# A hand-written plan of 1,494 steps is put into a new order on every engine

## The chip, the core and the metric

The kernel runs on one core of a Trainium2 chip. A core has five engines with a queue each: TensorE (PE, with its weight loads shown apart as PEld), VectorE (DVE), ScalarE (ACT), GpSimd (POOL) and SyncE (SP, which issues DMAs). Each takes its instructions in the order in which the program gives them, and waits on semaphores for the other engines. The metric is the device time of one execution in microseconds, and less is better.

## The reference

Inputs are `q`, `k`, `v` of shape (8 batches, 8 heads, 576 positions, 64), float32. First a linear attention with a "hedgehog" feature map, then a gate with a long convolution over the positions:

```
phi(x):  p = x @ w_phi (64 -> 128);  p -= max|p| per row;  [exp(p), exp(-p)]
kv = phi(k)^T v ; z = sum phi(k) ; attn = (phi(q) kv) / (phi(q) z)
x  = attn, heads side by side              # (8, 576, 512)
x1, x2, x3 = split(x @ w_proj)             # 512 -> 3 x 512
conv = irfft(rfft(x2) * rfft(filter_fft))  # along the 576 positions
out  = (x1 * conv * x3) @ w_out
```

## The kernel before

The kernel handles the eight batches one after another in a software pipeline: while the convolution of batch b runs, the attention of batches b+1 and b+2 is on its way. Everything is bfloat16 with float32 accumulation in PSUM, which has eight banks; most steps use a pair of them.

A batch goes through these steps (b is the batch, v or m one of four tiles of 128):

- `load` brings `q`, `k`, `v` in over POOL's DMA queue; `trh` transposes q and k by DMA on SP. For batch 0 `pt` (PE) and `pte` transpose instead, and `loadh` loads halves.
- `Qn`, `Pk` (PE) project q and k; `maxq`, `maxk` (DVE, line 710) reduce the absolute maximum; `ex` (ACT, line 696) takes the exponentials straight from PSUM. `Pq` projects q a second time, transposed, with the maximum (`mhi`, `mlo`, `trm`, `trme`) subtracted.
- `em` (ACT) and `vs` (POOL, line 752, `vp` and `vm`) scale v; `KV` (PE) sums k-features times v; `NE` (PE, line 781) applies it to q; `rc`, `xn` (DVE) divide. A small remainder of the positions goes the same way under names with a t (`Pkt`, `NEt`, `rct`, `xnt`).
- `trx`, `trxt` (SP) transpose the result by DMA to `xT`; `X1`, `X3` (PE, line 922) multiply with two thirds of `w_proj`.
- `f1` (line 849, `SD<-xn`) and `f2` (line 855, `xf<-SD`) are the butterfly sums ahead of the Fourier transform; each is on POOL or DVE. `F` (PE, lines 861 and 865) is the transform, `Fe` copies it out, `Xl` gathers a rest, `X2` (PE, line 900) multiplies with the last third of `w_proj`, `Y1` (DVE, lines 905, 910) multiplies with the filter's spectrum, and `m3` (line 914, `T<-T,T`) adds two products.
- `I` (PE, line 975) goes back to positions; `Ie` (ACT), `Ip` and `Im` (DVE, line 996) form sums and differences `cv`; `tm` (DVE) multiplies x1 and x3; `ym` (line 1041, `yT<-cv,x1s`) is the gate, on POOL or DVE; `J` and `yj` (line 1035) do the same for one tile with another transform. `yt` copies the rest.
- `O` (PE, line 1052) multiplies with `w_out`, `Oe` copies to one of four buffers `o0` to `o3`, `st` stores half a buffer from SP or, for the last batch, also from ACT.

Ahead of this the kernel makes the Fourier matrices from counters (`ang`, `frac`, `sin`), the filter's spectrum (`fl_load`, `fa`, `rev`, `fb`, `Ff`, `H`, `He`), and a few small constants (`one`, lines 354 and 355). `wz` steps (line 317) are matmuls on zeros whose result nobody reads.

Nothing is scheduled by the compiler: the text `PLAN` lists the steps, `name,arguments@bank`, and `run` calls them in this order, so the plan is the order of every queue and the choice of bank, and for many steps the first argument is the engine. Semaphores come from the data that the steps touch, so another order does the same work and waits in other places.

Of the kernel before, what the change touches and what calls it, by code (L numbers as in the profile page):

```python
# [37 lines left out]
wz,2@2 maxq,0,0@4 pt,q,0,1,0@0 sin,2 Pk,0,0@1 pte,ACT,q,0,1,1@3 fa,POOL,1 pt,k,0,1,0@6 maxk,0,0@1
pte,ACT,q,0,1,0@0 Qn,0,2@4 pt,k,0,1,1@0 maxq,0,2@4 pt,k,0,0,1@3 ex,k,p,0,0@1 load,k,1
pte,DVE,k,0,1,1@0 Qn,0,3@4 pte,DVE,k,0,1,0@6 ex,k,m,0,0@1 fa,POOL,0 wz,9@0 one Pk,0,3@6 maxq,0,3@4  # L40
pte,ACT,k,0,0,1@3 Pk,0,2@0 ex,k,m,0,3@6 Qnt,0@2 Pk,0,1@4 maxqt,0@2 ex,k,p,0,3@6 maxk,0,1@4 rev@2
ex,k,p,0,2@0 maxk,0,3@6 ex,k,p,0,1@4 maxk,0,2@0 Pkt,0@6 mhi,0 ex,k,m,0,1@4 trh,q,1,0 mlo,DVE,0
maxkt,0@6 ex,k,m,0,2@0 trm,0@4 wz,24@5 trme,DVE,0@4 fb,0@2 fl_loadt Pq,0,1@4 exkt,p,0@6 trh,q,1,1
exkt,m,0@6 wz,28@0 em,m,0,0 em,p,0,0 em,p,0,1 ex,q,m,0,1@4 vs,DVE,m,0,0 vs,POOL,p,0,0 Pq,0,2@6
ex,q,p,0,1@4 trh,k,1,0 fb,1@2 Pq,0,3@0 ex,q,m,0,2@6 Qn,1,0@4 wz,5@2 maxq,1,0@4 ex,q,m,0,3@0
trh,k,1,1 ft,POOL KV,0,0@2 ex,q,p,0,2@6 load,q,2 vs,DVE,p,0,1 em,m,0,1 ex,q,p,0,3@0 Qn,1,3@4
vs,POOL,m,0,1 maxq,1,3@4 Pk,1,1@6 KVe,ACT,0,0@2 Ff,0@0 ex,k,p,1,1@6 NE,0,1@2 Pq,0,0@4 Ffe,ACT,0@0
rc,0,1@2 gen_ends,POOL xn,0,1@2 ex,q,m,0,0@4 Pk,1,0@0 maxk,1,1@6 KV,0,1@2 trx,0,1 ex,q,p,0,0@4
load,v,1 maxk,1,0@0 ex,k,m,1,1@6 w_load,proj,2 NE,0,0@4 KVe,DVE,0,1@2 ex,k,m,1,0@0 load,k,2
rc,0,0@4 NE,0,2@2 xn,0,0@4 ex,k,p,1,0@0 Ff,1@6 rc,0,2@2 f1,POOL,0,0,1 xn,0,2@2 Qn,1,2@4 Ffe,ACT,1@6  # L50
ptx,0,0@0 maxq,1,2@4 Pqt,0@2 ptxe,ACT,0,0@0 f1,POOL,0,0,0 NE,0,3@6 exqt,p,0@2 Ff,3@0 rc,0,3@6
exqt,m,0@2 Ff,2@4 xn,0,3@6 Ffe,ACT,3@0 Pkt,1@2 f2,DVE,0,0,0 f1,POOL,0,1,1 Ffe,ACT,2@4 ptx,0,3@6
maxkt,1@2 Qn,1,1@0 ptxe,ACT,0,3@6 NEt,0@4 maxq,1,1@0 exkt,m,1@2 ptx,0,2@7 w_load,proj,1 exkt,p,1@2
ptxe,DVE,0,2@7 Hl,ACT f2,POOL,0,0,1 Qnt,1@0 Pk,1,2@2 maxqt,1@0 X1,0,2@7 ex,k,m,1,2@2 rct,0@4
f1,POOL,0,1,0 xnt,0,0@4 Pk,1,3@0 xnt,0,1@4 em,m,1,0 X1,0,3@6 ex,k,m,1,3@0 maxk,1,2@2 f2,POOL,0,1,0
# [6 lines left out]
vs,POOL,m,1,1 ex,k,m,2,1@0 late Y1,0,2@5 X2,0,3@6 ex,k,m,2,0@2 X1,0,1@0 mlo,DVE,1 load,k,3
ex,k,p,2,0@2 Y1,0,3@6 X2,0,1@5 load,q,3 Xl,ACT,0 trm,1@1 X3,0,1@2 Y1,0,0@4 trme,ACT,1@1 m3,POOL,0,1
X1e,ACT,0,1@0 Pq,1,1@6 Y1,0,1@5 Pkt,2@0 X2,0,4@4 ex,q,m,1,1@6 maxkt,2@0 m3,POOL,0,0 X3,0,0@5
ex,q,p,1,1@6 Y1,0,4@4 X1t,0@3 tm,0,1@2 exkt,m,2@0 X3t,0@4 exkt,p,2@0 tm,0,0@5 Pq,1,0@6 em,p,2,0
w_load,out X1te,ACT,0@3 Qn,2,3@0 tmt,0@4 KV,1,1@2 ex,q,p,1,0@6 vs,POOL,p,2,0 maxq,2,3@0
ex,q,m,1,0@6 Pq,1,2@4 KVe,DVE,1,1@2 Qn,2,1@0 ex,q,m,1,2@4 NE,1,0@6 maxq,2,1@0 load,k,4 X3,0,2@2
# [6 lines left out]
f1,POOL,1,1,1 NEt,1@4 trx,1,3 Oe,ACT,0,0@1 f1,DVE,1,1,0 O,0,3@0 ex,k,p,2,3@2 maxqt,2@6
f2,POOL,1,1,0 O,0,2@1 rct,1@4 xnt,1,0@4 ex,k,m,2,3@2 xnt,1,1@4 f2,DVE,1,1,1 Ft,1,1,6@4 trxt,1
em,m,2,1 Oe,DVE,0,2@1 em,p,2,1 Qn,3,2@2 Fs,1,3@6 maxq,3,2@2 Fs,1,2@4 X1,1,3@1 Fe,ACT,1,3@6
st,SP,0,1,0 Fe,ACT,1,2@4 trh,k,3,1 F,1,0@6 X1e,ACT,1,3@1 F,1,1@4 Oe,ACT,0,3@0 Qn,2,2@1 Fe,ACT,1,0@6
Fe,DVE,1,1@4 st,SP,0,3,1 X1,1,2@0 maxq,2,2@1 trh,k,3,0 X2,1,0@4 X2,1,2@5 mhi,2 X1e,ACT,1,2@0
st,SP,0,0,1 mlo,POOL,2 vs,POOL,m,2,1 st,SP,0,2,0 trm,2@0 X3,1,0@1 Y1,1,2@5 trme,ACT,2@0 trh,q,3,0
# [1038 lines left out]
```

## Time and profile before

| what | value |
|---|---|
| time, median of the runs | 311.26 us |
| lowest of the runs | 310.44 us |
| span of the profiled execution, first to last instruction | 309.5 us |
| median less span (what lies around the span) | 1.8 us |
| PE busy | 281.9 us, 91% |
| DVE busy | 270.8 us, 88% |
| ACT busy | 219.7 us, 71% |
| POOL busy | 201.8 us, 65% |

The profile is of one execution. The page gives busy time by engine; the groups give the mean duration of each kind of instruction; the windows give busy time in a stretch; the timeline shows the rows one after another, where rows of a kind that follow each other are merged ("x3"). An idle time in square brackets stands with what ended it.

### The profile page before, as it was taken

The page shows a single profiled execution, that of the slowest core. Times are in us where ns is not written, and L with a number is a line of the kernel's source. Part 1 is how long each engine was busy: PE and PEld are TensorE (multiplying, and loading weights), DVE is VectorE, ACT ScalarE, POOL GpSimd, SP SyncE. Part 2 cuts the span into 40 slices and gives each one's busy share as a digit, 9 for nine tenths or more (in the row PEclk, how much of TensorE's full clock was granted, in tenths as well). Part 3 has the DMA queues.
Part 4 walks back from the last instruction along what each step waited for, and adds up shares of the span by engine and source line. Part 5 has one row for each costly group of instructions (what it writes and reads, how often), then busy time and mean ns, then how long its engine had stood idle before and what let it go on. Part 6 is the DMA issues. An engine that isn't in the chain of part 4 may idle for free.

```text
span 309.5 us, 10297 instructions
## 1 busy us (share of the span) xinstructions
PE 281.9 (91%) x4337; PEld 203.6 (66%) x4364; DVE 270.8 (88%) x451; ACT 219.7 (71%) x354; POOL 201.8 (65%) x160
## 2 busy tenths in 40 slices
PE   8558888999999999999599899899999999999993
PEld 3333657688568777676358767577487766886661
DVE  6999999999979896999899897878999888797963
ACT  1988999896749895899338768977657898924120
POOL 8253879998558748949445369957699619773040
PEclk9977999999999999999799999999999999999998
DMA  7999799999599994999929976962756142041236
GB/s 147 229 208 180 97 173 162 147 210 178 89 181 200 132 182 108 135 142 159 179 27 216 131 105 135 160 113 59 114 130 118 32 103 54 2 69 32 65 78 196
DMA packets 72191, 40.07 MB, mean 129 GB/s; under 512 B 52496, under 2 KB 66960, under 8 KB 72144
## 3 DMA queue, kind: packets, MB, share of 16 engines
q1 hardware_dynamic: 56928, 22.49, 40.2%
q0 software_dynamic: 14816, 16.25, 33.4%
q8 instruction: 34, 0.56, 0.8%
q10 hardware_dynamic: 400, 0.66, 0.7%
q14 instruction: 13, 0.11, 0.1%
HBM read 33.75 MB, written 9.44 MB: 140 GB/s over the span
## 4 chain that ended last, share of the span: by engine, by line
PE 72%; DVE 12%; issue 5%; ACT 5%; DMA 4%; POOL 0%; SPq 0%; DVEq 0%; POOLq 0%; ACTq 0%
PE ps L922 16%; PE ps L900 10%; PE ps L1052 8%; PE ps L767 6%; PE ps L781 5%; PE ps L975 5%; DMA xT<-xn 3%; PE ps L931 3%; PE ps L1031 3%; PE ps L861 2%; PE ps L641 2%; PE ps L668 2%; PE ps L865 2%; PE ps L634 2%; PE ps L674 2%
## 5 line engine op out<-in xcount | busy, mean ns | idle before, releaser
L922 PE MATMUL ps<-xT,wproj 128*128 128x256 bf16 x512 | 64.9, 273 | 0.8 <-DMA xT<-xn 0.8
L922 PEld LDWEIGHTS <-wproj 128*128 128x128 bf16 x512 | 48.5, 98 | 11.4 <-issue 1.8
L752 POOL TENSOR_TENSOR vp<-vn,vp 128x1152 bf16<-128x1152 bf16 x15 | 33.3, 2228 | 23.6 <-ACT vp L746 23.4
L710 DVE TENSOR_REDUCE mq<-ps 128x8 f32<-128x1024 f32 (+1 forms) x40 | 43.9, 1112 | 5.0 <-PE ps L649 2.6
L710 DVE TENSOR_REDUCE mk<-ps 128x8 f32<-128x1024 f32 (+1 forms) x40 | 44.0, 1111 | 2.7 <-PE ps L649 1.8
L1041 POOL TENSOR_TENSOR yT<-cv,x1s 128x576 bf16<-128x576 f32 x23 | 29.1, 1280 | 21.8 <-DVE cv L996 19.9
L849 POOL TENSOR_TENSOR SD<-xn 128x512 bf16<-128x512 bf16 x23 | 26.6, 1167 | 23.0 <-DVE xn L800 22.1
L752 POOL TENSOR_TENSOR vm<-vn,vm 128x1152 bf16<-128x1152 bf16 x15 | 32.9, 2191 | 8.4 <-ACT vm L746 8.4
L696 ACT ACTIVATE Eqm<-ps 128x1024 bf16<-128x1024 f32 x32 | 32.4, 1027 | 6.7 <-PE ps L674 6.6
L696 ACT ACTIVATE Ekp<-ps 128x1024 bf16<-128x1024 f32 x32 | 32.8, 1038 | 4.5 <-DVE mk L710 3.0
L1052 PE MATMUL ps<-wout,yT 128*128 128x512 bf16 x131 | 34.9, 387 | 1.2 <-issue 0.4
L696 ACT ACTIVATE Eqp<-ps 128x1024 bf16<-128x1024 f32 x32 | 32.6, 1029 | 3.8 <-PE ps L674 3.6
L696 ACT ACTIVATE Ekm<-ps 128x1024 bf16<-128x1024 f32 x32 | 32.9, 1035 | 1.8 <-PE ps L634 1.5
L900 PE MATMUL ps<-wproj,XF 128*128 128x512 bf16 x121 | 30.0, 379 | 0.6 <-issue 0.3
L914 POOL TENSOR_TENSOR T<-T,T 128x1024 bf16<-128x1024 bf16 x13 | 27.6, 2131 | 4.1 <-DVE T L910 4.1
L298 ACT CAST x1s<-ps 128x512 bf16<-128x512 f32 (+1 forms) x31 | 16.3, 536 | 17.5 <-PE ps L931 9.7
L910 DVE TENSOR_TENSOR T<-ps,HTo 128x1024 bf16<-128x1024 f32 x16 | 19.5, 1219 | 5.0 <-PE ps L900 5.0
L855 POOL TENSOR_TENSOR xf<-SD 128x512 bf16<-128x512 bf16 x19 | 21.9, 1167 | 2.8 <-DVE SD L849 2.4
L800 DVE TENSOR_TENSOR xn<-ps,r 128x512 bf16<-128x512 f32 x32 | 22.0, 690 | 1.1
L963 DVE TENSOR_TENSOR x1s<-ps,x1s 128x512 bf16<-128x512 f32 x32 | 21.4, 682 | 0.9 <-ACT XF L298 0.5
L1052 PEld LDWEIGHTS <-yT 128*128 128x128 bf16 x144 | 13.3, 99 | 13.4 <-issue 1.4
L298 ACT COPY o<-ps 128x512 f32<-128x512 f32 x24 | 14.4, 601 | 9.4 <-PE ps L1052 9.4
(179 smaller groups left out, 689.7 us busy)
## 6 DMA issues: line engine op xcount, KB each, us to landing
out_dram<-o SPq DMA_DIRECT2D x67, 128.0 KB, 2.5
vn<-in_v_dram POOLq DMA_DIRECT2D x8, 576.0 KB, 8.1
qn<-in_q_dram POOLq DMA_DIRECT2D x7, 576.0 KB, 8.1
kn<-in_k_dram POOLq DMA_DIRECT2D x7, 576.0 KB, 8.5
wproj<-in_moe_w_proj_dram POOLq DMA_DIRECT2D x3, 512.0 KB, 10.1
fl<-in_moe_filter_fft_dram SPq DMA_DIRECT2D x8, 128.0 KB, 6.4
out_dram<-o ACTq DMA_DIRECT2D x5, 128.0 KB, 2.9
qn<-in_q_dram POOLq DMA_DIRECT2D x2, 288.0 KB, 7.1
```

The source lines that it names most:

```text
L298: self.nc.scalar.copy(dst, src)
L696: self.nc.scalar.activation(e, p, AF.Exp, bias=0.0, scale=1.0 if g == "p" else -1.0)
L710: self.nc.vector.tensor_reduce(out=out, in_=src, axis=AX.X, op=ALU.max, apply_absolute_value=True)
L752: self.eng(eng).tensor_tensor(out=t[:, :, :, 0:64], in0=self.at("vn", b)[:, 2 * X:2 * X + 2], in1=t[:, :, :, 64:65].to_broadcast([128, 2, ...
L800: self.nc.vector.tensor_tensor(out=o, in0=n[:, :, :, 0:64], in1=self.at("r", 4 * b + v).to_broadcast([128, 2, 4, 64]), op=ALU.mult)
L849: self.eng(eng).tensor_tensor(out=o[:, :, 2 * i:2 * i + 2, :], in0=x[:, :, 0:2, :], in1=x[:, :, 2:4, :], op=ALU.subtract if i else ALU.add)
L855: self.eng(eng).tensor_tensor(out=o[:, :, 2 * i:2 * i + 2, :], in0=x[:, :, 0:4:2, :], in1=x[:, :, 1:4:2, :], op=ALU.subtract if i else ALU ...
L900: self.mm(self.pb(0), l, w[:, kt, 512:1024], start=(kt == 0), stop=(kt == 3))
L914: self.eng(eng).tensor_tensor(out=Y, in0=Y, in1=self.at(f"T{2 * e + 1}", b), op=ALU.add)
L922: self.mm(o[:, d], w[:, kt, f0 + 128 * m:f0 + 128 * m + 128], y[:, 1, ::-1, ::-1] if d else y[:, 0], start=(kt == 0), stop=(kt == 3))
L1041: self.eng(eng).tensor_tensor(out=self.at("yT", b)[:, m, 0:SEQ], in0=self.turn_of("cv", (b, m)).rearrange("p x h t -> p (x h t)"), in1=sel ...
L1052: self.mm(self.pb(0), y[:, kt, 128 * c:128 * c + 128], w[:, kt, :], start=(kt == 0), stop=(kt == 3))
```

## The change

Only the table `PLAN` changes. It holds as many steps as before, 1,494, and the same work: the same 16 `wz` steps and the same loads and stores. What differs is the order, on all five queues; the PSUM banks that many steps use; and the engine of 78 steps that copy, add or multiply (`Fe`, `Oe`, `X1e`, `KVe`, `Xl`, `f1`, `f2`, `m3`, `ym`, `mlo`, `trme`, `vs`, `yt`). On DVE the net is: `ym` 1 to 4 steps, `m3` 3 to 5, `f1` 9 to 10, `f2` 13 to 11, `trme` 3 to 6, `Oe` 12 to 13, `Xl` 3 to 4, and one less of `X1e`, `KVe` and `yt`. Of the loads of the filter (`fl_load`) most stand in the text behind the first loads of q and k.

```diff
-fl_load,0,1 gz,DVE loadh,q,0,0 zeros wz,14@0 w_load,phi gi_part loadh,k,0,0 wz,17@1 ident cols_m
...
+fl_loadt fl_load,0,0 w_load,phi gi_part gz,DVE wz,5@0 wz,27@1 cols_m zeros cols_i fl_load,3,0
+loadh,q,0,0 ident pt,q,0,0,0@1 loadh,k,0,0 fl_load,1,0 gi_nr ang,3 pt,q,0,0,1@0 fl_load,3,1 cols_f
...
```

Three places show what moves. Row numbers of the source are three lower in the changed kernel, since its table is three lines shorter (L855 before is L852 after). The first place is DVE in the convolution of batch 3: `SD` is written by `f1`, `xf` by `f2`, `cv` by `Ip` and `Im`, `mk` by `maxk`, `rt` and `xnt` by `rct` and `xnt`. Before:

```order
L710 TENSOR_REDUCE mk_85<-ps 128x2x4
L996 TENSOR_TENSOR cv_1121<-es_1119,ps 128x9x32 x2
L1035 TENSOR_TENSOR yT_1122<-ps,x1s_140 128x2x9x32
L300 CAST x1s_140<-ps 128x2x8x32
L849 TENSOR_TENSOR SD_136<-xn_129 128x2x256
L855 TENSOR_TENSOR xf_137<-SD_136 128x2x256 x3
L806 RECIPROCAL rt_128<-ps 128x8
L812 TENSOR_TENSOR xnt_131<-ps,rt_128 64x256 x2
```

And in the changed kernel, for the same batch:

```order
L993 TENSOR_TENSOR cv_1134<-es_1132,ps 128x9x32
L993 TENSOR_TENSOR cv_1133<-es_1131,ps 128x9x32
L846 TENSOR_TENSOR SD_136<-xn_129 128x2x256
L993 TENSOR_TENSOR cv_1133<-es_1131,ps 128x9x32
L707 TENSOR_REDUCE mk_85<-ps 128x2x4
L993 TENSOR_TENSOR cv_1134<-es_1132,ps 128x9x32
L852 TENSOR_TENSOR xf_137<-SD_136 128x2x256
L993 TENSOR_TENSOR cv_1134<-es_1132,ps 128x9x32
L1032 TENSOR_TENSOR yT_1135<-ps,x1s_140 128x2x9x32
L803 RECIPROCAL rt_128<-ps 128x8
```

One `f2` of batch 3 is left on DVE instead of three, and it and the one `f1` now stand among the half sums of batch 2. The second place is POOL beside it, with its DMA issues. Before:

```order
L1041 TENSOR_TENSOR yT_1122<-cv_1120,x1s_140 128x576
L1041 TENSOR_TENSOR yT_1122<-cv_1121,x1s_140 128x576
L593 DMA qn_75<-in_q_dram 128x4x576
L593 DMA vn_80<-in_v_dram 128x4x576
L752 TENSOR_TENSOR vp_106<-vn_79,vp_106 128x18x64
L855 TENSOR_TENSOR xf_137<-SD_136 128x2x256
```

In the changed kernel:

```order
L911 TENSOR_TENSOR T_1126<-T_1126,T_1127 128x1024
L590 DMA vn_79<-in_v_dram 128x4x576
L846 TENSOR_TENSOR SD_136<-xn_129 128x2x256 x3
L852 TENSOR_TENSOR xf_137<-SD_136 128x2x256
L1038 TENSOR_TENSOR yT_1135<-cv_1134,x1s_140 128x576
L1038 TENSOR_TENSOR yT_1135<-cv_1133,x1s_140 128x576
L590 DMA qn_75<-in_q_dram 128x4x576
L852 TENSOR_TENSOR xf_137<-SD_136 128x2x256
```

The butterflies of batch 3 have gone from DVE to POOL, and the load of v and an `m3` stand ahead of them there. The third place is the end of ACT's queue, where `o0` to `o3` are the output buffers and each DMA stores half of one. Before:

```order
L298 COPY o2_1126<-ps_61 128x512
L298 COPY o3_1127<-ps_61 128x512
L1061 DMA out_0_dram<-o3_1127 64x512
L1061 DMA out_0_dram<-o0_1124 64x512
L1061 DMA out_0_dram<-o1_1125 64x512
L1061 DMA out_0_dram<-o2_1126 64x512
L1061 DMA out_0_dram<-o3_1127 64x512
```

In the changed kernel, where DVE fills `o3`, `o0` and `o2` ahead of the last copy:

```order
L295 COPY yT0_1135<-yT1_1136 128x4x64
L1058 DMA out_0_dram<-o0_1137 64x512
L295 COPY o1_1138<-ps_61 128x512
L1058 DMA out_0_dram<-o3_1140 64x512
L1058 DMA out_0_dram<-o1_1138 64x512
L295 COPY o3_1140<-ps_61 128x512
L1058 DMA out_0_dram<-o2_1139 64x512
L1058 DMA out_0_dram<-o3_1140 64x512
```

In both the last copy (into `o3`) reuses the buffer of the first output tile of batch 7. Before, half of that tile was ACT's first store; now the store stands behind another store and behind a copy that waits for PE.

More of the change, by code (lines that the diff above doesn't have):

```diff
@@ L38 @@
[L38 to L43, printed above, removed]
@@ L62 @@
[L62 to L67, printed above, removed]
@@ L74 @@
[L74 to L79, printed above, removed]
@@ new lines @@
+Fe,ACT,0,3@4 mlo,DVE,1 w_load,out vs,POOL,m,1,1 He,ACT,1,1@2 He,DVE,4,0@1 X1,0,2@0 X1e,ACT,0,2@0
+Pk,2,1@4 KV,1,0@6 load,v,2 Pk,2,0@0 He,ACT,1,0@2 maxk,2,1@4 em,p,1,1 X3,0,0@3 trm,1@2 Xl,DVE,0
+maxk,2,0@0 trxt,0 KVe,ACT,1,0@6 ex,k,p,2,1@4 X2,0,2@6 late trme,DVE,1@2 X2,0,1@2 ex,k,m,2,1@4
+X3,0,1@7 X2,0,3@4 load,k,3 ex,k,m,2,0@0 ex,k,p,2,0@0 Y1,0,2@6 tm,0,0@3 Pq,1,1@5 Y1,0,1@2
+ex,q,p,1,1@5 tm,0,1@7 ex,q,m,1,1@5 Pkt,2@0 trh,q,2,0 trh,q,2,1 load,q,3 maxkt,2@0 X1t,0@2 X2,0,0@3
+Y1,0,3@4 exkt,m,2@0 X1te,ACT,0@2 X2,0,4@7 exkt,p,2@0 vs,POOL,p,1,1 Y1,0,0@3 KV,1,1@4 m3,POOL,0,1
```

298 lines of the change are left out of this document (153 added, 145 removed).

## Prediction

> **What bounds the kernel now.** I read the busy times first, then stretches of time, then who waited for whom, and last the rows around the worst wait.
>
> ```profile
> span 309.5 us, 10297 instructions
> PE 281.9 (91%) x4337; PEld 203.6 (66%) x4364; DVE 270.8 (88%) x451; ACT 219.7 (71%) x354; POOL 201.8 (65%) x160
> ```
>
> PE and DVE are both nearly full. The work is the same in the changed kernel, so the time can only change where PE stands idle or runs at a lower clock, which is at most 309.5 - 281.9 = 27.6 us. The windows (PE, PEld, DVE, ACT, POOL busy, then granted clock and DMA share) say where that is:
>
> ```profile
> 0.00:50.00 50.00, 38.31 (x552) 23.36 (x556) 45.08 (x103) 40.99 (x63) 31.78 (x39) 0.93 1.03 175
> 50.00:140.00 90.00, 88.20 (x1502) 66.31 (x1509) 81.67 (x125) 71.49 (x117) 68.65 (x51) 1.00 0.95 153
> 140.00:150.00 10.00, 6.28 (x66) 4.72 (x64) 9.92 (x13) 6.86 (x11) 8.39 (x7) 0.98 0.99 163
> 150.00:160.00 10.00, 9.80 (x70) 5.89 (x72) 8.83 (x12) 4.41 (x9) 4.86 (x3) 0.85 0.44 88
> 160.00:300.00 140.00, 134.97 (x2135) 101.56 (x2146) 122.40 (x198) 95.02 (x155) 88.08 (x63) 1.00 0.55 96
> ```
>
> Start-up (first 50 us) leaves PE idle 11.7 us, and part of its 38.31 us are the zero matmuls. The steady part, 230 us, leaves only 1.8 + 5.0 = 6.8 us. One window of 10 us loses 3.7 us by itself, with DVE full, and the clock falls behind it. PE's longest wait and the rows of DVE, POOL and PE there:
>
> ```profile
> PE ps L861 <- DVE xnt L812: 3.8, 1, 3.8
> 143.35 0.43 DVE L849 TENSOR_TENSOR SD<-xn 128x512 bf16<-128x512 bf16 x1
> 143.81 5.27 DVE L855 TENSOR_TENSOR xf<-SD 128x512 bf16<-128x512 bf16 x3
> 149.23 0.43 DVE L812 TENSOR_TENSOR xnt<-ps,rt 64x256 bf16<-64x256 f32 x1
> 143.44 0.81 POOL L593 DMA_DIRECT2D qn<-in_q_dram  x1
> 144.24 0.75 POOL L593 DMA_DIRECT2D vn<-in_v_dram  x1
> 145.00 2.17 POOL L752 TENSOR_TENSOR vp<-vn,vp 128x1152 bf16<-128x1152 bf16 x1
> 147.10 1.35 POOL L855 TENSOR_TENSOR xf<-SD 128x512 bf16<-128x512 bf16 x1
> 150.15 0.66 PE L861 MATMUL ps<-Dt,xnt 128*128 128x288 bf16 x2 [3.82 <-DVE xnt L812]
> L855 DVE TENSOR_TENSOR xf<-SD x13: 371/416/3649, 43.3 to 254.1; 128x512 bf16<-128x512 bf16 x13
> ```
>
> Three `f2` of batch 3 took 5.27 us on DVE, though one has a median of 0.416 us (the last row: minimum, median, maximum in ns): the first sat for 3.649 us while POOL went through two load issues and a `vs`. DVE was held, `rct` and `xnt` stood behind it, and `F` on PE waited 3.82 us. I call this a hold.
>
> **The hold goes: -5.3 us.** In the changed plan two of the three `f2` are POOL's, and those ahead of `xnt` now stand among half sums. Without the hold, three `f2` (1.25 us), `rct` and two `xnt` (1.1 us) from 143.8 end at 146.1, about when PE ran out of work (150.15 - 3.82 = 146.33), so the whole 3.82 us goes. The clock of 0.85 in the next 10 us cost 0.15 x 10 = 1.5 us more. Bounds: -3.8 (the clock falls for another reason) to -5.3; I take -5.3.
>
> The Trainium skill, page TensorE: Matmul & The Clock Gate, section Part 1: The HAM clock gate (the "warmup" mystery), says that PE drops to half clock after an idle window of about 3.4 us. The trace agrees: a wait of 3.82 us is followed by the window at 0.85. By that rule shorter waits lose only themselves.
>
> **Holds come back elsewhere: +2.5 us.** What was held was an addition on DVE with both inputs in SBUF, against POOL. Counted in the change, such steps (`f1`, `f2`, `m3`, `ym`) go from 26 to 30 on DVE. At batch 3 POOL's queue now has, in a row, `m3`, a load, three `f1`, an `f2` and a `ym`: by the rows below 2.13 + 0.8 + 3 x 1.17 + 1.17 + 1.28 = 8.9 us without a break, and DVE's `f1` and `f2` of batch 3 arrive in it. Each waits at most for the operation under way, about 1.2 us, so 2 x 1.2 = 2.4 us. From below 0 (POOL has run ahead and is free); from above a repeat of the hold, 5.3. I take 2.5, nearer to the rows of the train itself.
>
> ```profile
> L914 POOL TENSOR_TENSOR T<-T,T 128x1024 bf16<-128x1024 bf16 x13 | 27.6, 2131 | 4.1 <-DVE T L910 4.1
> L849 POOL TENSOR_TENSOR SD<-xn 128x512 bf16<-128x512 bf16 x23 | 26.6, 1167 | 23.0 <-DVE xn L800 22.1 <-DVE yT L300 0.9
> L1041 POOL TENSOR_TENSOR yT<-cv,x1s 128x576 bf16<-128x576 f32 x23 | 29.1, 1280 | 21.8 <-DVE cv L996 19.9 <-DVE x1s L967 1.6
> L914 DVE TENSOR_TENSOR T<-T,T 128x1024 bf16<-128x1024 bf16 x3 | 2.0, 680 | 0.0
> L1041 DVE TENSOR_TENSOR yT<-cv,x1s 128x576 bf16<-128x576 f32 x1 | 0.8, 759 | 0.0
> L300 DVE COPY o<-ps 128x512 f32<-128x512 f32 x12 | 8.2, 686 | 2.4 <-PE ps L1052 2.0 <-DMA out_dram<-o 0.3
> L849 DVE TENSOR_TENSOR SD<-xn 128x512 bf16<-128x512 bf16 x9 | 3.7, 424 | 0.1
> ```
>
> The Trainium skill, page SBUF — State Buffer, section Who interferes with whom, says that a VectorE instruction with two SBUF inputs contends with a GpSimd instruction that reads SBUF, and infers that generating DMA descriptors does not hold such a one. The rows agree on the first and speak against the second: the `f2` issued at 143.81 was still held from 143.81 to 145.00, when POOL did nothing but issue loads. By the page's inference loads ahead of a DVE step cost nothing, and the train above would be 0.8 us shorter.
>
> **DVE gets more work: +3.0 us.** Net of the 78 steps, DVE gains two `m3` (2 x 0.68 = 1.36) and three `ym` (3 x 0.76 = 2.28), and one `f1` more against two `f2` less is -0.42. The copies cancel at about 0.69 each, and three small `trme` less a `KVe` end near nothing. Sum +3.2 us. POOL's relief hides: no PE wait on POOL is over 0.3 us. DVE's 3.2 us could hide in its 38.7 us of idle time, hence bounds 0 to 3.2. I take 3.0, since from 50 to 140 us DVE is busy 81.67 of 90 us while PE has only 1.8 us idle, so little is hidden.
>
> **The end: +1.8 us.** The rows there (the copies to `o`, a store from ACT, and what a store takes):
>
> ```profile
> 299.07 0.76 DVE L1035 TENSOR_TENSOR yT<-ps,x1s 128x576 bf16<-128x576 f32 x1
> 299.88 4.48 PE L1052 MATMUL ps<-wout,yT 128*128 128x512 bf16 x20 [0.15 <-DVE yT L1035]
> 300.94 0.59 ACT L298 COPY o<-ps 128x512 f32<-128x512 f32 x1 [0.59 <-PE ps L1052]
> 301.56 4.21 ACTq L1061 DMA_DIRECT2D out_dram<-o  x5
> 304.55 0.69 DVE L300 COPY o<-ps 128x512 f32<-128x512 f32 x1 [0.27 <-DMA out_dram<-o]
> DMA to landing us min/median/max: 2.2/2.7/3.1
> ```
>
> Before, PE waited 0.15 us for the last `yj` and began the five `O` of batch 7 at 299.88; the buffer of the first was stored from ACT at 301.56, 1.7 us on, and the last copy began at 304.55, 4.67 us on, 0.27 us late. In the changed plan a `ym` on DVE (0.76) stands ahead of the last `yj`, after the last `I`, which delays that `O` by about 0.9 us. And the first buffer's second half is stored by ACT only behind another store, which waits for the second copy: 1.06 + 2 x 0.86 + 0.69 less the overlap puts that first store at 2.6, so the one for `o3` at 3.2, landing 2.7 later at 5.9 instead of 4.67, less 0.3 at the faster landings: +0.9. Together 1.8; bounds 0.5 (only the `ym`, half hidden) to 2.8 (a landing of 3.1 and both copies late).
>
> **The start: -0.5 us.** Before, the constant `one` was held on DVE, too, by POOL's `fa`, and PE waited behind it:
>
> ```profile
> 18.00 2.15 DVE L354 TENSOR_TENSOR onex<-ident 128x36 bf16<-128x36 bf16 x1
> 17.75 2.36 POOL L491 TENSOR_TENSOR turn<-fl 128x1024 f32<-128x1024 f32 x1
> 16.94 1.02 ACT L696 ACTIVATE Ekp<-ps 128x1024 bf16<-128x1024 f32 x1
> 2.43 4.13 SPq L479 DMA_DIRECT2D fl<-in_moe_filter_fft_dram  x7
> PE ps L634 <- DVE mq L710: 1.9, 1, 1.9
> ```
>
> Now `one` comes early, when POOL computes nothing: -1.9. Against that, two counters stand ahead of POOL's first load, and ACT has one more copy ahead of the first exponential (16.94 before), some +1.4. Whether the loads of the filter stand before or behind in the text is of little account: SP issued all of them by 6.56 us without waiting for POOL, and SP's order has them first in both. Their price I bound from the first 50 us: -3 to +2.
>
> **All other places: 0.** The steady part's 6.8 us of idle time could vanish or double: -6.8 to +6.8. No row says which, so I take nothing.
>
> Sum: -5.3 + 2.5 + 3.0 + 1.8 - 0.5 = +1.5 us on the profiled 309.5, so a span of 311.0. The median of the runs is 1.8 us above the span; carried over, 312.8 us.
>
> **Rivals.**
>
> *No new hold, and a shorter start.* -5.3 from the old hold, +0.5 at the end, -3 at the start and DVE's work hidden: 311.3 - 7.8 = 303.5 us. For it: 28 of the 31 additions and SBUF copies on DVE found POOL idle or won, so the order before mostly kept them apart. Against: four more of them, with POOL trains as long.
>
> *A hold that halves the clock.* The slower case: a DVE addition comes upon the POOL train of batch 3, or the similar one of batch 5 (`m3`, three `f1`, two `f2`), and `Ip`, `Im` and `xnt` stand behind it. It decides once PE idles over about 3.8 us, as at 146: each such place costs 5.3. With two of them, 311.3 - 5.3 + 10.6 + 3.0 + 1.8 = 321.4 us. For it: DVE is 91% busy and cannot catch up. Against: arrivals are spread, and two holds of 1.2 us stay below that point.
>
> *The filter loads do nothing.* If "behind the first inputs" were real, the inputs would land sooner; by SP's rows it is not. The time is the forecast's, 312.8; I give it 0.8 and it does not change the sum.
>
> **Chances.** The forecast and what lies within 2% of 311.3 (305.0 to 317.5) has 0.50, the first rival 0.15, the second 0.35. Two per cent, 6.2 us, is about what a measurement of this kernel can tell from no change. The range takes in both rivals and the bounds of the steady part as far as they are likely: 304 to 323.
>
> **What would show it.** Right: no PE wait near 3.8 us; DVE rows L846, L852, L1038 or L911 longer than twice their median beside POOL rows; DVE busy near 274 us; the last copy waiting for a DMA over 0.5 us; `one` under 0.5 us. Wrong: PE idle in 50 to 300 us clearly under 5 or over 15 us, or a start that is more than 3 us off.

## The result: 9% slower, and DVE's SBUF steps now meet POOL's

The changed kernel took 341.6 us (median of four runs, 338.6 to 347.5), the kernel before beside it 313.5 us (310.4, 311.3, 315.6 and one run of 462.2): a ratio of 1.094, with a 95% interval of 1.087 to 1.101. Forecast was 312.8 us with a range of 304 to 323. The profiled execution is the longest of the four (345.7 us; the others span 336.8 to 340.6), so the sums made on it are about 6 us too large for the median.

The page after, and the windows that were shown of before (PE, PEld, DVE, ACT, POOL busy, then granted clock and DMA):

```profile
span 345.7 us, 10288 instructions
PE 293.5 (85%) x4332; PEld 209.6 (61%) x4364; DVE 296.5 (86%) x457; ACT 220.3 (64%) x353; POOL 195.9 (57%) x156
```

```profile
0.00:50.00 50.00, 33.86 (x479) 21.68 (x483) 40.72 (x93) 35.78 (x51) 25.43 (x35) 0.90 1.13 172
50.00:140.00 90.00, 78.30 (x1163) 57.40 (x1171) 81.81 (x110) 62.51 (x105) 57.88 (x43) 0.94 0.76 122
140.00:150.00 10.00, 8.31 (x69) 4.35 (x68) 10.00 (x11) 4.55 (x7) 5.43 (x3) 1.00 1.22 188
150.00:160.00 10.00, 9.27 (x288) 7.96 (x287) 8.61 (x15) 6.23 (x8) 2.87 (x2) 1.00 0.50 75
160.00:300.00 140.00, 126.03 (x1888) 91.17 (x1903) 121.60 (x176) 98.13 (x161) 89.70 (x65) 0.98 0.61 101
```

Of the 36.2 us between the two profiles, 24.6 us are more idle time of PE (52.2 against 27.6) and 11.6 us are longer busy time of PE for the same matmuls, most of it at a lower clock. In a profile of the same order with one store moved (337.9 us, below) the two parts are 19.5 and 8.9 us. The stretch from 50 to 140 us, which idled for 1.8 us, now idles for 11.7 us, while DVE is as busy in it as before and does less. The loss is spread over many places: the clock is 0.90, 0.94 and 0.98 in the long windows, against 0.93, 1.00 and 1.00 before.

DVE's busy time rose by 25.7 us, though its added work is 3.2 us by the prediction's rows. The groups of DVE that have all their inputs in SBUF show the rest (busy, mean ns of one):

```profile
L846 DVE TENSOR_TENSOR SD<-xn 128x512 bf16<-128x512 bf16 x10 | 12.8, 1282 | 0.2
L852 DVE TENSOR_TENSOR xf<-SD 128x512 bf16<-128x512 bf16 x11 | 10.2, 923 | 0.0
L749 DVE TENSOR_TENSOR vm<-vn,vm 128x1152 bf16<-128x1152 bf16 x2 | 8.3, 4157 | 0.0
L911 DVE TENSOR_TENSOR T<-T,T 128x1024 bf16<-128x1024 bf16 x5 | 6.3, 1260 | 0.0
L297 DVE COPY XL<-XF 128x512 bf16<-128x512 bf16 x4 | 5.7, 1415 | 0.0
L731 DVE TENSOR_TENSOR mh<-mq,mh 128x36 bf16<-128x36 f32 x3 | 4.4, 1470 | 0.3 <-ACT mh L727 0.3
```

On average an `f1` took 0.424 us before and 1.282 here, an `m3` 0.680 and 1.260. Counted row by row (`f1`, `f2`, `m3`, `ym`, `vs`, `mlo`, `Xl`, `yt` and `one`), 23 of 41 such steps were held, which means here longer by over a tenth than a step of their kind that is alone, for 31 us in all; before it was 5 of 37, for 7.5 us. Each of the 23 began while a POOL operation or load issue was under way. In the profile with one store moved it is again 23 of 41, for 32 us. The longest waits of PE:

```profile
PE ps L764 <- DVE vm L749: 4.1, 1, 4.1
PE ps L612 <- DMA qn<-in_q_dram: 3.7, 1, 3.7
PE ps L858 <- DVE o L297: 3.6, 1, 3.6
PE ps L919 <- DVE xT L297: 3.1, 1, 3.1
PE ps L764 <- issue: 4.2, 2, 2.9
PE ps L897 <- DVE mT L297: 2.9, 1, 2.9
```

Three of the six (behind `vm`, `xT` and `mT`) stand behind a held DVE step; the one behind `o` stands behind a store, and the one with `issue` is a stop inside `KV`. The first of them, in the timeline (start, duration):

```profile
26.59 2.17 POOL L749 TENSOR_TENSOR vp<-vn,vp 128x1152 bf16<-128x1152 bf16 x1
28.57 5.61 DVE L749 TENSOR_TENSOR vm<-vn,vm 128x1152 bf16<-128x1152 bf16 x1
28.70 2.15 POOL L749 TENSOR_TENSOR vm<-vn,vm 128x1152 bf16<-128x1152 bf16 x1
30.80 2.15 POOL L749 TENSOR_TENSOR vp<-vn,vp 128x1152 bf16<-128x1152 bf16 x1
34.23 0.62 PE L764 MATMUL ps<-vm,Ekm 64*128 64x65 bf16 x16 [4.07 <-DVE vm L749]
```

DVE's `vs` came 0.2 us before the end of POOL's first `vs` and got through only when POOL's train of three had ended at 32.95 us: 5.61 us for a step that takes 1.35. `ft`, `maxq` and `KVe` stood behind it on DVE, and `KV` on PE waited 4.07 us.

### The profile page after: what moved, and what is told of

The parts are those of the page before. It is cut to its first block, busy times and chain, and to the rows that moved or that the text cites. A ratio compares the mean times of both kernels' runs of the same rounds, so it can differ in the third digit from the quotient of the medians.

```text
span 345.7 us, 10288 instructions
## 1 busy us (share of the span) xinstructions
PE 293.5 (85%) x4332; PEld 209.6 (61%) x4364; DVE 296.5 (86%) x457; ACT 220.3 (64%) x353; POOL 195.9 (57%) x156
## 4 chain that ended last, share of the span: by engine, by line
PE 49%; DVE 24%; issue 10%; DMA 6%; ACT 5%; POOL 4%; SPq 1%; ACTq 0%; DVEq 0%; POOLq 0%
PE ps L919 10%; PE ps L897 8%; PE ps L764 6%; PE ps L778 5%; DMA out_dram<-o 3%; DVE mk L707 3%; PE ps L1049 3%; PE ps L972 3%; DVE mq L707 3%; PE ps L665 2%; PE ps L928 2%; PE ps L1028 2%; DMA xT<-xn 2%; DVE xf L852 2%; DVE vm L749 2%
## 5 line engine op out<-in xcount | busy, mean ns | idle before, releaser
L919 PE MATMUL ps<-xT,wproj 128*128 128x256 bf16 x512 | 68.1, 281 | 6.5 <-DVE xT L297 3.1
L919 PEld LDWEIGHTS <-wproj 128*128 128x128 bf16 x512 | 49.6, 101 | 19.6 <-issue 6.9
L707 DVE TENSOR_REDUCE mk<-ps 128x8 f32<-128x1024 f32 (+1 forms) x40 | 43.9, 1109 | 4.6 <-PE ps L631 2.6
L749 POOL TENSOR_TENSOR vp<-vn,vp 128x1152 bf16<-128x1152 bf16 x16 | 35.7, 2234 | 10.9 <-ACT vp L743 10.9
L911 POOL TENSOR_TENSOR T<-T,T 128x1024 bf16<-128x1024 bf16 x11 | 23.2, 2124 | 28.1 <-DVE T L907 28.1
L897 PE MATMUL ps<-wproj,XF 128*128 128x512 bf16 x116 | 32.4, 394 | 4.7 <-DVE mT L297 2.9
L1038 POOL TENSOR_TENSOR yT<-cv,x1s 128x576 bf16<-128x576 f32 x20 | 25.9, 1310 | 17.2 <-DVE cv L993 13.1
L749 POOL TENSOR_TENSOR vm<-vn,vm 128x1152 bf16<-128x1152 bf16 x14 | 30.0, 2151 | 5.7 <-ACT vm L743 5.7
L852 POOL TENSOR_TENSOR xf<-SD 128x512 bf16<-128x512 bf16 x21 | 24.8, 1191 | 7.0 <-DVE SD L846 6.1
L972 PE MATMUL ps<-inv,T 128*128 128x288 bf16 x144 | 20.6, 286 | 1.8 <-DVE mq L707 1.1
L897 PEld LDWEIGHTS <-XF 128*128 128x128 bf16 x128 | 12.0, 100 | 16.2 <-issue 6.2
```

Source lines behind the costliest of these rows:

```text
L707: self.nc.vector.tensor_reduce(out=out, in_=src, axis=AX.X, op=ALU.max, apply_absolute_value=True)
L749: self.eng(eng).tensor_tensor(out=t[:, :, :, 0:64], in0=self.at("vn", b)[:, 2 * X:2 * X + 2], in1=t[:, :, :, 64:65].to_broadcast([128, 2, ...
L852: self.eng(eng).tensor_tensor(out=o[:, :, 2 * i:2 * i + 2, :], in0=x[:, :, 0:4:2, :], in1=x[:, :, 1:4:2, :], op=ALU.subtract if i else ALU ...
L897: self.mm(self.pb(0), l, w[:, kt, 512:1024], start=(kt == 0), stop=(kt == 3))
L911: self.eng(eng).tensor_tensor(out=Y, in0=Y, in1=self.at(f"T{2 * e + 1}", b), op=ALU.add)
L919: self.mm(o[:, d], w[:, kt, f0 + 128 * m:f0 + 128 * m + 128], y[:, 1, ::-1, ::-1] if d else y[:, 0], start=(kt == 0), stop=(kt == 3))
```

## The experiments

**What holds DVE, measured by itself.** A probe behind the end of the kernel before: six stages in which DVE does eight operations while POOL works through a train.

```diff
+            if s == 1:
+                for n, b in (("q", 0), ("q", 1), ("k", 0), ("k", 1)):
+                    self.load(n, b)
...
+                for _ in range(5):
+                    add(nc.gpsimd, pg, plain)
+            for _ in range(8):
+                if s in (0, 1):
+                    add(nc.vector, pd, plain)
```

> The kernel before with a probe behind it, in six stages that wait for each other; its time means nothing. DVE does eight operations against a train of POOL: (0) additions of two SBUF tiles against additions; (1) the same against four load issues; (2) half sums with one input in PSUM against additions; (3) copies from SBUF to SBUF against additions; (4) reductions from PSUM against additions; (5) copies against two load issues. Theory (a hold lasts until POOL's operation or train ends, whatever POOL does): in 0, 1, 3 and 5 single DVE operations take 1 us or more instead of 0.42 (in 1 and 5 by 0.7 us and more), in 2 and 4 none. Rival (load issues do not hold DVE): in 1 and 5 all stay below 0.5 us.

The groups of stages 2, 4 and 3 (minimum, median, maximum in ns), and stage 1 in the timeline:

```profile
L1096 DVE TENSOR_TENSOR cv<-es,ps x8: 445/453/455, 318.0 to 321.4; 128x288 f32<-128x288 f32 x8
L710 DVE TENSOR_REDUCE mk<-ps x8: 1218/1224/1224, 334.5 to 343.3; 128x8 f32<-128x1024 f32 x8
L1100 DVE COPY pd<-xn x8: 293/1157/1193, 326.8 to 333.5; 128x512 bf16<-128x512 bf16 x8
```

```profile
313.65 1.52 POOL L593 DMA_DIRECT2D kn<-in_k_dram  x2
313.86 1.26 DVE L1074 TENSOR_TENSOR pd<-xn 128x512 bf16<-128x512 bf16 x1
```

With one input in PSUM nothing is held (445 to 455 ns against POOL's additions, reductions 1218 to 1224). From SBUF to SBUF even a copy with a single input is: five of eight took four times their 293 ns. And an addition of 0.42 us took 1.26 us while POOL did nothing but issue loads, though three others of that stage passed at full speed during the issues; in stage 5 a copy took 1.41 us in the same way. So the theory stands, load issues included, with one correction: in the probe POOL's operations follow each other 0.08 us apart and DVE gets in behind one of them, whereas in the kernel, where the next POOL row starts without a gap, it waited for two or three.

**Order or engines.** The new order with the old engines, and the old order with the new ones (98 steps, counted step by step; the 78 of the change leave some of them out).

```diff
 new order, old engines:            old order, new engines:
-f1,DVE,0,1,1                      -f1,POOL,0,1,1
+f1,POOL,0,1,1                     +f1,DVE,0,1,1
...
```

> The order and banks of the changed plan, with every copy, addition and product on the engine it had before (98 steps set back, counted step by step). Theory (holds: DVE additions, copies and products between SBUF tiles come upon POOL's operations because the new order makes them meet): the old engines in the new order meet POOL as well, so DVE keeps at least 10 us of held time and the time stays over 325 us. Rival (the new engines do it, by more such steps on DVE): DVE's busy time falls to about 270 us and the time comes back to within 2% of the kernel before, 305 to 320 us.

> The order and banks of the plan before, with the 98 steps on the engines of the changed plan. Theory (holds from the order): some new holds, 315 to 330 us, well under the changed kernel. Rival (engines): 335 us or more. If both this one and the one with old engines are slow, order and engines fit each other only in pairs, and neither half carries the loss by itself.

Measured: 356.8 us (ratio 1.142, 1.135 to 1.148) and 331.8 us (1.064, 1.061 to 1.068). Neither half is harmless, and the first is slower than the change as a whole. The rival of the first falls, and so does the simple form of the theory: the old order is only good with its own engines. In the second, 12 of 41 steps were held, for 12.4 us. In the first, the slowest of all, it is only 8 of 37, for 14.7 us, and DVE's busy time is down to 279.0 us, while PE idles for 59.7 us:

```profile
PE 295.9 (83%) x4364; PEld 210.2 (59%) x4364; DVE 279.0 (78%) x451; ACT 220.4 (62%) x355; POOL 200.0 (56%) x160
```

So holds on DVE don't explain that kernel: among its longest PE waits two stand behind held `f2` (4.9 and 3.1 us), but others are for the first q (4.5), a transposed q (3.1), POOL's `vs` (3.1) and a stop inside `KV` (3.3). Order and engines fit in pairs, and what the new order costs without its engines stays open. The order goes with its PSUM banks in all these runs, and no run separates the two.

**No such step on DVE, in both orders.**

```diff
-f1,DVE,0,1,1
+f1,POOL,0,1,1
-Xl,DVE,0
+Xl,ACT,0
...
```

> The changed plan with every f1, f2, m3, ym, vs and mlo of DVE given to POOL and every Xl and yt of DVE to ACT (40 steps): DVE has nothing left that was held. Theory (holds): DVE falls from 296 to about 250 us, no DVE row is over twice its median, the time falls to 310 to 328 us although POOL rises from 196 to about 240 us. Rival (stores, loads and the start are what is late): the time stays at 335 us or more.

> The plan before with the same rule as in the run without additions on DVE: all its f1, f2, m3, ym, vs and mlo of DVE go to POOL, its Xl and yt of DVE to ACT. Neither order has holds then, so the two runs differ by order and banks alone. Theory (holds carry nearly all of the loss): this kernel is within 2% of the changed plan without additions on DVE, which took 330 us, so 324 to 336 us. Rival (the new order loses by itself, by its start, stores and loads): it stays near the kernel before, 310 to 318 us.

Measured: 330.3 us for the new order (1.056, 1.050 to 1.062) and 314.2 us for the old one (1.011, 1.005 to 1.017). The first gained 11 us, less than expected; the second lost only 3. By the bounds set beforehand the rival of the second holds, and at face value 16 us belong to the order. But the first run was not free of holds: `ft`, a copy of the filter's last row that was left on DVE, now met the train of `vs` itself. And POOL, with 236 us of work in both, was late in its turn: PE waited for it up to 3.5 us in the new order and up to 3.0 us in the old one, against 0.4 us in the changed kernel.

```profile
L297 DVE CAST f<-flt 64x512 bf16<-64x512 f32 x1 | 6.2, 6159 | 0.0
```

```profile
PE ps L862 <- POOL xf L852: 3.5, 5, 1.4
PE ps L509 <- DVE f L297: 3.2, 1, 3.2
PE ps L1049 <- POOL yT L1038: 2.4, 3, 1.6
PE ps L735 <- POOL mh L731: 2.0, 1, 2.0
```

This pair speaks against holds as nearly the whole loss, but removing them in this way puts POOL on the path, so it doesn't give the order's own price.

**Single places.** Three held steps of batch 0 set elsewhere; one of them only moved; four places mended (the moved `vs`, `ptxe` ahead of the held `f1`, `Xl` on ACT, one store); that store alone.

```diff
 three holds:                    vs early:
-vs,DVE,m,0,0                    em,p,0,0
+vs,POOL,m,0,0                  +vs,DVE,m,0,0
-f1,DVE,0,1,1                    exkt,p,0@4 wz,4@6 trme,DVE,0@7
+f1,POOL,0,1,1                   ...
-Xl,DVE,0                        fb,0@2 ex,q,p,0,1@4
+Xl,ACT,0                       -vs,DVE,m,0,0
 four places, and the store alone:
 st,SP,1,4,1
+st,SP,1,4,0
 ...
 trh,q,5,1
-st,SP,1,4,0
```

> The changed plan with three steps set elsewhere: vs of batch 0 (m, 0) and f1 of batch 0 (1, 1) to POOL, Xl of batch 0 to ACT. Their holds took 5.61, 3.43 and 2.87 us, and PE waited 4.07, 3.08 and 2.91 us behind them, each followed by the clock at 0.5 (13.7 us in all, worth half of it). Theory: without them 10.1 us of waiting and up to 6.8 us of clock go, so the time falls by 10 to 17 us, to 324 to 331 us. Rival (PE would have waited there anyway, for POOL's slower steps or for loads): the time falls by under 5 us.

Measured: 342.4 us, no gain. The theory of additive places falls. The three holds were gone, and others stood there: `ft` took 6.85 us, and a `f2` came upon two `f2` and a `vs`:

```profile
56.06 5.22 DVE L852 TENSOR_TENSOR xf<-SD 128x512 bf16<-128x512 bf16 x1
56.64 2.25 POOL L852 TENSOR_TENSOR xf<-SD 128x512 bf16<-128x512 bf16 x2
58.86 2.14 POOL L749 TENSOR_TENSOR vp<-vn,vp 128x1152 bf16<-128x1152 bf16 x1
61.34 0.66 PE L862 MATMUL ps<-D,xf 128*128 128x144 bf16 x4 [4.92 <-DVE xf L852]
```

> The changed plan with one step moved and no engine changed: vs of batch 0 on DVE (m, 0), which was held for 5.61 us behind three vs of POOL, stands ahead of trme and fb, where DVE was idle (25.2 to 26.2 us) and POOL had not begun its vs. Theory (this hold makes the late start): the step takes 1.3 us, KV of batch 0 ends 4 to 6 us earlier than 43.9 us, and if nothing later absorbs it the time falls by 4 to 8 us, to 333 to 337 us. Rival (the meetings behind it come out anew and cost as much, as when the three holds of batch 0 were taken out): KV of batch 0 is earlier, but the time stays at 338 to 344 us.

Measured: the moved step took 1.35 us, and `KV` of batch 0 ended at 38.2 us instead of 43.9 (before: 37.8), as expected. The time was 340.0 us with runs from 332.5 to 345.5: what was won there is within the spread of the whole.

> The changed plan with four places mended: vs of batch 0 on DVE ahead of trme and fb (as in the run before); ptxe of batch 0 (2) ahead of the f1 that was held; Xl of batch 0 on ACT; the store of output tile (1, 4, half 0) ahead of two DMA transposes. Their waits on PE were 4.07, 3.08, 2.91 and 3.61 us, each with the clock at half behind it. Theory (places add up): the four waits are gone and the time falls by 14 to 22 us, to 318 to 326 us. Rival (with other arrival times new holds take their place): 330 us or more.

Measured: 332.8 us (1.063, 1.055 to 1.071), runs from 331.0 to 334.3. All four waits were gone and four new ones of 1.5 to 2.5 us had come ahead of 60 us; 21 of 40 steps were still held, for 24.3 us. A gain of 9 us where 14 to 22 were expected.

> The changed plan with one step moved: the store of output tile (1, 4, half 0) stands ahead of the DMA transposes of q for batch 5 and not behind them. In four profiles of this order its landing took 6.8 to 14.7 us, against a median of 2.5 us, and PE waited 1.57 to 9.71 us behind it. Theory: the wait at F of batch 3 (2) is under 1 us, the time falls by 2 to 6 us to 336 to 340 us, and the runs lie closer together than before (338.6 to 347.5, and 332.5 to 345.5 with vs moved). Rival (the store is late for another reason): the wait and the spread stay.

Measured: 339.8 us, runs from 338.0 to 339.9. The wait at `F` of batch 3 was gone and the gain is about 2 us. The four runs lay close together, as they do with four places mended, which moves this store as well (331.0 to 334.3). That it alone spreads the times isn't shown: two kernels below that move it too run from 317.9 to 324.8 and from 317.4 to 323.1 us. Where the store stood behind two DMA transposes of q, its landing differed from execution to execution. The landings of that stretch in two executions of the order, first of the changed kernel:

```profile
DMA to landing us min/median/max: 2.2/2.5/8.6
```

and of the kernel of the next experiment, where PE waited 9.71 us for it:

```profile
DMA to landing us min/median/max: 2.2/2.7/14.7
```

**The wait inside `KV` of batch 5.**

```diff
-load,v,6
 ...
 m3,POOL,4,0
+load,v,6
```

> The changed plan with the load of v for batch 6 behind m3 of batch 4 on POOL. PE stood for 2.88 us in the middle of KV of batch 5 (1), at 226.18 us, with nothing to wait for in the program, 1.3 us behind the issue of that load (before: 1.40 us at the same step). Theory (PE's instructions come by DMA, behind the load's 576 KB): the wait at that step falls to 1.4 us or less. Rival (the load has no part in it): it stays at 2.5 us or more.

Measured in one execution: 2.51 us at that step, just inside the rival's bound, and other kernels of this order that keep the load in place have 2.4 to 3.0 us there: this load is not seen to be the cause. A wait stands at this step in the kernels of both orders (1.15 us without additions on DVE in the old order, 3.3 us in the new order with the old engines), and the traces show nothing that ends it; its cause stays open.

**POOL's work shortened, in both orders.** This leaves the order and the engines alone: on POOL `vs`, `f1`, `f2` and `m3` do a quarter of their columns and leave out the rest, so what holds DVE is shorter. POOL's own results come earlier as well, but in the changed kernel PE never waited for POOL for more than 0.4 us. A first pair zeroed its buffers at the start.

```diff
+        w = 32 if eng == "POOL" else 128
-        self.eng(eng).tensor_tensor(out=o[:, :, 2 * i:2 * i + 2, :], in0=x[:, :, 0:2, :],
-                                    in1=x[:, :, 2:4, :], op=ALU.subtract if i else ALU.add)
+        self.eng(eng).tensor_tensor(out=o[:, :, 2 * i:2 * i + 2, 0:w], in0=x[:, :, 0:2, 0:w],
+                                    in1=x[:, :, 2:4, 0:w], op=ALU.subtract if i else ALU.add)
```

> The changed plan, with work left out: POOL's vs, f1, f2 and m3 do only a quarter of their columns (the rest keeps old values; four kinds of buffer are set to zero once at the start on POOL, ahead of fa). No step moves and no engine changes, but what can hold DVE lasts about 0.35 to 0.6 us instead of 1.2 to 2.2. Theory (holds, and the clock behind them, carry most of the 30 us): DVE's busy time falls from 296 to about 272 us and the time to 312 to 322 us. Rival (the order loses in other places, stores, transposes and the start): 328 us or more.

> The plan before with the same work left out on POOL. Theory (holds): it gains little, since it has one large hold and a small one: 303 to 311 us, and the difference from the changed plan with a quarter of POOL's work is under 12 us. Rival (the order by itself): the difference between the two stays at 20 us or more.

Measured: 331.8 and 324.0 us. The difference of 8 us is what the theory expects, but both times are far above it, since the zeroing spoiled the pair: it took POOL 10 us ahead of `fa` and held DVE as well, whose `ang`, a scaling with one input in SBUF, stood against eight fills that read nothing:

```profile
6.80 10.81 DVE L422 TENSOR_SCALAR turn<-fr,cols 128x288 f32<-128x288 f32 x2
7.49 3.15 POOL L490 MEMSET vp<- 128x1170 bf16 x3
10.52 3.15 POOL L490 MEMSET vm<- 128x1170 bf16 x3
```

The second pair leaves `f1` and `f2` of the first batch and `vs` of the first two whole instead.

```diff
+        w = 32 if eng == "POOL" and b > 0 else 128
```

> The changed plan with the same kind of work left out, but without the zeroing at the start, which took POOL 10 us ahead of fa and spoiled the pair before: vs of batches 0 and 1 and f1, f2 of batch 0 are whole, later ones and all m3 on POOL do a quarter of their columns. Up to KV of batch 1 (80.8 us in the changed kernel, 67.6 us before) the start with its holds stays as it is; behind it the changed kernel needs 264.9 us to its end and the kernel before 241.9 us. Theory (holds): behind KV of batch 1 this one is within 6 us of its pair. Rival (the order by itself): 12 us or more stay there.

> The plan before with the same work left out. Theory (holds): 303 to 311 us in all, since only the hold at 146 us goes; behind KV of batch 1 within 6 us of the changed plan with the same work. Rival: 12 us or more between the two behind KV of batch 1.

Measured: 326.3 us (1.040, 1.030 to 1.051) for the new order, 312.3 us (1.006, 1.002 to 1.010) for the old. In the profiles, `KV` of batch 1 ended at 76.7 and 67.9 us, and from there the new order needed 243.1 us and the old one 242.4 us. The windows of the two, new order first:

```profile
50.00:140.00 90.00, 82.57 (x1261) 60.13 (x1262) 81.90 (x118) 63.24 (x104) 36.12 (x42) 0.96 0.88 138
140.00:300.00 160.00, 154.40 (x2474) 113.98 (x2467) 142.71 (x226) 112.67 (x182) 50.43 (x75) 1.00 0.57 101
```

```profile
50.00:140.00 90.00, 84.62 (x1419) 62.94 (x1417) 76.24 (x115) 66.84 (x109) 36.59 (x47) 0.98 0.92 148
140.00:300.00 160.00, 155.65 (x2372) 115.74 (x2371) 142.36 (x230) 110.85 (x182) 54.10 (x75) 1.00 0.61 103
```

Behind batch 1 the profiles differ by 0.7 us, where those of the full kernels differ by 23 us (264.9 and 241.9). The new order's profile is the fastest of its four executions, 4.7 us under their median, so on medians some 5 us may be left. With POOL's operations short the two orders are nearly equal there: most of the loss behind the start goes with the length of POOL's operations, as it would if it were the holds and what follows from them. The old order did not gain, as it was expected to: a wait of 4.04 us on PE at `Qn` of batch 3 came in place of the hold.

What is left, 14 us in the medians, lies for the most part in the start: 8.8 us up to `KV` of batch 1 in the profiles.

```diff
 the four places of above, and POOL's work shortened; then also:
-ft,POOL
+ft,ACT
```

The plan's `ft,POOL` runs on DVE, since `copy` uses DVE for all that is not ACT's.

> The four mended places (vs, ptxe and Xl of batch 0, the store of tile 1, 4) and the shortened work of POOL (as in the pair g3 and g4) in one kernel, on the changed plan. Theory (holds and the late store are the whole loss): what was left of the start, 8.8 us up to KV of batch 1, goes as well, and the time is within 2% of the plan before with the same work left out (312.3 us): 306 to 318 us. Rival (the new order's start is slower by itself): 319 us or more.

> The kernel with four mended places and POOL's later work shortened, and ft (the copy of the filter's last row, one input in SBUF) on ACT. With vs of batch 0 out of its way, ft on DVE was held behind the train of vs of batch 0 itself: it took 4.46 us there, 6.16 us in the run without additions on DVE and 6.85 us where three holds of batch 0 were taken out, against 0.59 us in the changed kernel, and PE waited 2.15 us for it. Theory (the rest of the late start is this hold): KV of batch 1 ends 2 to 4 us earlier than 72.8 us, and the time falls from 318.7 to 313 to 317 us. Rival (the start of the new order is slower by itself): the time stays at 318 us or more.

Measured: 318.7 us (1.025, 1.020 to 1.029) and 320.4 us (1.033, 1.026 to 1.041). The four places were worth 7.6 us; `ft` nothing that can be seen in the time, though `KV` of batch 1 ended at 71.5 instead of 72.8 us. Both stay 6 to 8 us above the old order with the same work; the first lies between the bounds of its theory and its rival, and the theory of the last run falls. Batch 0 is whole in all of these, and an `f1` and an `f2` of it were still held in the last run, where they took 2.66 and 1.93 us; whether these or the start's order itself make the rest wasn't separated.

**The hold at 146 us of the kernel before.** One step moved, and then all `f2` of batch 3 on POOL.

```diff
 one step ahead:                 all four on POOL:
+f2,POOL,3,0,1                  +f2,POOL,3,1,1 f2,POOL,3,1,0 f2,POOL,3,0,0 f2,POOL,3,0,1
 load,q,6                        load,q,6
 ...                             ...
 vs,POOL,p,4,0                  -f2,DVE,3,1,1 ... f2,DVE,3,0,0 ... f2,DVE,3,1,0
-f2,POOL,3,0,1                  -f2,POOL,3,0,1
```

> The kernel before with one step moved: f2 of batch 3 on POOL (0, 1) stands ahead of the loads of q and v and of vs, so that the three f2 on DVE come upon load issues and not upon a vs of 2.17 us. Theory (the hold at 146 us and the clock behind it cost 5.3 us): the wait of 3.82 us falls under 1 us and the time falls by 3 to 5.3 us, to 306 to 308.5 us. Rival (load issues hold DVE until the operation behind them has ended): the wait stays at 3 us or more and the time within 1 us of the kernel before.

> The kernel before with the three f2 of batch 3 that DVE had given to POOL, all four ahead of the loads of q and v and of vs: DVE has nothing to be held there. Theory: POOL ends the two that F needs first at about 146.2 us, when PE runs out of work, the wait of 3.82 us falls under 1 us, the clock stays up, and the time falls by 3 to 5 us to 306 to 308 us, below both kernels. Rival (vs of batch 4, 4.7 us later, or POOL's slower f2 is late in its place): within 1 us of the kernel before.

The first gave 311.2 us (1.002, 0.998 to 1.006): its rival holds. The first `f2` got through behind POOL's `f2`, and the next took from 145.50 to 149.26 us, over two load issues and the `vs` that follows them without a gap. The second gave 307.5 us (0.981, 0.974 to 0.988), below both kernels. POOL's four `f2` there, and `F`:

```profile
143.75 4.49 POOL L855 TENSOR_TENSOR xf<-SD 128x512 bf16<-128x512 bf16 x4 [0.45 <-DVE SD L849]
144.68 0.86 DVE L812 TENSOR_TENSOR xnt<-ps,rt 64x256 bf16<-64x256 f32 x2
145.97 0.41 PE L861 MATMUL ps<-Dt,xnt 128*128 128x288 bf16 x2
```

An `f2` takes 1.15 us on POOL and 0.42 on DVE, and the kernel is still 6 us faster with the slow ones, since nothing meets there.

## Why the prediction was wrong

**The hold at 146 us** was right, in cause and price: taken away by itself in the kernel before, it gave 5.9 us (1.9% of 313.5, with an interval of 3.7 to 8.1) where 3.8 to 5.3 were expected. In the changed kernel the long hold is gone there too: the `f1` and `f2` of batch 3 left on DVE took 0.99 and 0.87 us, which is 1.0 us of holding where 2.4 were forecast.

**"Holds come back elsewhere: +2.5 us (0 to 5.3)" is the step that failed.** They came back at 23 steps and not at two, for 31 us of DVE's time; 15 us of the kernel's time went when POOL's later operations were shortened, and part of the late start comes on top. Two mistakes are in it. First, I counted additions, 26 before and 30 after, and looked at one place; `mlo`, `vs`, `Xl` and `ft` can be held as well, and all 41 steps are dealt anew when the order changes. Second, the old order's few holds (28 of 31 steps had passed freely) served as the rate to expect, and nothing says that another order keeps it. POOL computes for 57% of the span, so of 41 steps that arrive at any moment 23 would meet it, and 23 did; but that agreement is of this order with its own engines only. The same product gives 24 for the kernel before, where 5 were held, 24 for the old order with the new engines (12) and 21 for the new order with the old ones (8). The pair with shortened POOL work shows the size: 15 of the 28 us went with the length of POOL's later operations alone. The rest isn't fully divided between holds of the start and the order itself.

**The second rival, "a hold that halves the clock", was the right mechanism** at 0.35, with a wrong number of places (two) and a wrong point for the clock. I wrote that it decides once PE idles over about 3.8 us. The windows of the changed kernel, in pairs of 3.41 us:

```profile
52.75:56.16 3.41, 0.63 (x16) 0.41 (x10) 3.38 (x2) 1.65 (x2) 3.04 (x3) 1.00 0.93 117
56.16:59.57 3.41, 3.11 (x17) 2.29 (x17) 3.41 (x5) 1.21 (x2) 3.41 (x3) 0.50 1.10 229
86.88:90.29 3.41, 1.54 (x20) 0.99 (x18) 3.41 (x6) 1.64 (x2) 1.95 (x2) 1.00 1.04 186
90.29:93.70 3.41, 3.41 (x33) 2.34 (x27) 2.58 (x4) 1.94 (x2) 2.20 (x2) 0.50 0.02 5
127.83:131.24 3.41, 1.64 (x16) 1.30 (x14) 3.02 (x3) 1.80 (x3) 3.41 (x4) 1.00 1.00 122
131.24:134.66 3.42, 3.36 (x37) 1.97 (x36) 2.35 (x3) 2.66 (x5) 3.40 (x4) 1.00 1.18 265
```

All changes of the clock lie on one grid of 3.41 us. PE was busy for 0.63 and 1.54 us of the first windows of the upper two pairs, and the whole next window ran at 0.50; for 1.64 us in the third, and the clock stayed. So a wait of 1.87 us (88.09 to 89.96 us) cost 1.7 us more, and one of 1.77 us nothing. Five windows behind held DVE steps ran at half clock, one behind the store, and two behind stops inside `KV` (of batches 0 and 5). The first rival, no new hold and a shorter start, fell with both of its parts.

**DVE's work, +3.0 us,** cannot be told from the holds in any run; DVE's unheld rows are as priced (`ym` 0.75, `m3` 0.68 us).

**The end, +1.8 us,** was within its bounds: the last copy waited 2.16 us for a store and the time from the last `O` to the end grew from 5.1 to 6.4 us. The `ym` ahead of the last `yj` cost nothing, since PE had the `O` of the batch before to do until then.

**The start, -0.5 us,** was right up to 28 us: `one` took 0.38 us, PE waited 3.7 us for the first q, and `Pq` of batch 0 began at 26.43 us against 27.24. Then the `vs` of batch 0 was held. The orders set `vs` and `fb` of DVE in another sequence there, and POOL's train of `vs` was not followed against it. At the end of `KV` of batch 1 the changed kernel was 13.2 us late (80.8 against 67.6 us), where the bounds were -3 to +2.

**All other places, 0:** here stand the store behind the transposes (3.61 us, and 0.8 to 9.7 in other executions), a wait for a DMA transpose of 1.77 us, and the stop inside `KV`, 1.5 us longer than before.

## What to carry over

Two engines that exclude each other make the order of a hand-written plan a fit in time, not only in sequence: how seldom steps met in the old order says little about a new one. The other engine's busy share times the steps that can be held gave about as many holds as there were in the changed kernel and two to five times too many in three others, so it is a bound for the bad case and no forecast. Mending single places of the changed kernel gained less than their waits, and new meetings came behind them. Shortening the long operations of the holding engine gained 15 us in the new order and nothing in the old one. Where a step's wait matters, the slower engine without a meeting can be the faster choice, as at the `f2` of batch 3. A wait on PE is priced with the window of 3.41 us in which it falls.

## What the runs showed of the hardware

- The clock of PE goes by how busy PE was in a window, not by the length of one wait. In the 19 profiles other than the probe's, cut into windows of 3.41 us on their own grids, every one of some 38 windows at full clock with PE busy under 40% was followed by one at half clock, about half of some 20 with 40 to 47%, about a fifth of some 65 with 47 to 62%, and none of some 1,500 above. The Trainium skill, page TensorE: Matmul & The Clock Gate, section Part 1: The HAM clock gate (the "warmup" mystery), gives the same window, free-running, and speaks of an idle one; the traces agree on the window, and show that one half idle is enough.
- A hold goes on over POOL operations that follow without a gap (5.61 us over three `vs`, 3.65 us over two load issues and a `vs`), and ends after one where 0.08 us lie between.
- POOL's fills hold DVE, too: 10 us of them kept two scalings with one input in SBUF for 10.8 us. The Trainium skill, page SBUF — State Buffer, section Who interferes with whom, says that copies and scalings have modes that contend with GpSimd, and that an instruction with at most one input in SBUF, outside these modes, does not; the probe's copies, and its additions and reductions from PSUM, agree with this. Its inference that load issues leave additions alone is spoken against by the probe's 1.26 us.
- A store of 128 KB behind DMA transposes landed after 6.8 to 14.7 us in four profiles of nearly the same order (at most three steps differ), against a median of 2.5 us.
